# Sliding-window attention with sinks, then a highway layer: two stages turned into one pipeline over 24 blocks of 128 tokens

## The chip, the core and the metric

The kernel runs on one core of a Trainium2 chip. A core has a matrix engine (PE), a vector engine (DVE), an activation engine (ACT), a GpSimd engine (POOL) and a sync engine (SP). PE writes its results to PSUM; DVE and ACT read them there and write to SBUF. In this kernel POOL's queue issues the loads, which turn float32 in memory into fp16 in SBUF, and SP's queue issues the stores. The metric is device time in microseconds; lower is better.

## The reference

```
scores = q @ k.T / 8        # 4 batches, 8 heads, 768 positions, head size 64
keep   = (key < 4) or (0 <= query - key < 128)
a      = softmax(where(keep, scores, -1e9))
x      = (a @ v)            # heads side by side: 3072 tokens x 512
H      = relu(x @ w_h)
T      = sigmoid(x @ w_t + b_t)
out    = T * H + (1 - T) * x    # float32, 3072 x 512
```

A query sees its own block of 128 keys (lower triangle), the block before it (upper triangle) and the first four keys, the sinks.

## The kernel before

Work is done in two stages, one after the other, each with its own PSUM pools.

The attention stage loops over 4 batches and, in each, over 4 head pairs (`attention`, L142). The tiles of q and k are loaded by token block (L108, L110), turned by PE (`transpose_qk`, L124 and L126) and copied by DVE to `qTt` and `kTt` (L128, L129); the turns of the next batch are put among the head pairs of this one, and a high priority offset lets the scheduler move them to where PE has nothing else. For a head pair, `qk_mms` makes scores of two key blocks at a time, each against two query blocks of 128 (L167, 64 rows high, 256 columns); ACT takes the exponential (L176) and DVE multiplies by the mask (L179, L182, L186). `sink_scores` makes the scores against the four sinks for all later blocks (L150, four output rows) and their exponential (L153). `av_mms` then forms the weighted sum for each block and head: the block before (L198), the own block (L202) and the sinks (L206), the last one with a contraction of four rows. The value tile has a column of ones, so that the sum of the weights comes out beside the result; DVE takes its reciprocal (L227) and scales (L228) into `x_tok`. PE turns that (L235) and ACT copies it to `xT` (L236).

The highway stage (L268) loops over 24 blocks of 128 tokens. PE makes eight matmuls of 512 columns (L273 with `w_h`, L276 with `w_t`) and adds the bias with a ninth whose contraction is one row (L279). ACT takes the sigmoid (L282), DVE makes relu minus x (L284), times T (L286), plus x (L288), and SP's queue stores the tile (L289). The weights are loaded by POOL's queue (L81, L83) behind the q and k of the third batch.

Of the kernel before, what the change touches and what calls it, by code (L numbers as in the profile page):

```python
# [19 lines left out]
def kernel(  # L21
# [11 lines left out]
):  # L33
    nc = tc.nc
# [11 lines left out]
    NSC = S // P  # L46
    NHP = H // 2
    NOC = DM // P
    SCALE = 1.0 / math.sqrt(D)

    const = ctx.enter_context(tc.tile_pool(name="const", bufs=1))
    xT_pool = ctx.enter_context(tc.tile_pool(name="xTp", bufs=1))
    xT = [xT_pool.tile([P, NT], FP16, tag=f"xT{hp}", name=f"xT{hp}")
          for hp in range(NHP)]
    x_tok = xT_pool.tile([P, NT // P, NHP, P], FP16, tag="x_tok", name="x_tok")

    ident = const.tile([P, P], FP16, tag="ident")
    make_identity(nc, ident)
    ebias = const.tile([P, 1], FP32, tag="ebias")
    nc.vector.memset(ebias, _EXP_BIAS)  # L60
    masks = {}
    for nm in ("mask_std", "mask0"):
        m = const.tile([P, 2, P], FP16, tag=nm, name=nm)
        nc.gpsimd.memset(m, 1.0)
        nc.gpsimd.affine_select(
            out=m[:, 0, :], in_=m[:, 0, :], compare_op=ALU.is_ge, fill=0.0,
            base=0, pattern=[[1, P]], channel_multiplier=-1)
        nc.gpsimd.affine_select(
            out=m[:, 1, :], in_=m[:, 1, :], compare_op=ALU.is_ge, fill=0.0,
            base=-1, pattern=[[-1, P]], channel_multiplier=1)  # L70
        masks[nm] = m
    nc.vector.memset(masks["mask0"][0:NSINK, :, :], 1.0)
    wh_sb = const.tile([P, NOC, DM], FP16, tag="wh")
    wt_sb = const.tile([P, NOC, DM], FP16, tag="wt")
    bt16 = const.tile([1, DM], FP16, tag="bt16")
    ones_row = const.tile([1, P], FP16, tag="ones_row")
    nc.vector.memset(ones_row, 1.0)

    def load_weights():
        with tc.high_priority(offset=_BULK):  # L80
            nc.gpsimd.dma_start(  # L81
                out=wh_sb, in_=moe_w_h.rearrange("(kc p) of -> p kc of", p=P))
            nc.gpsimd.dma_start(  # L83
                out=wt_sb, in_=moe_w_t.rearrange("(kc p) of -> p kc of", p=P))
# [249 lines left out]
```

## Time and profile before

| | |
|---|---|
| median of 3 runs | 206.18 us (204.13 to 206.53) |
| profiled execution, span of its instructions | 204.6 us |
| mean granted PE clock, share of 2.4 GHz | 0.736 |
| instructions | 3110 |

The profiled execution is recorded from its first instruction to its last; what lies around that span isn't recorded, and the median of the runs is 1.6 us above the span. Attention takes about the first 141 us, the highway stage the rest. Busy time counts an instruction from its start to its end; matmuls overlap, so that the distance between the starts of two neighbours, and not their length, tells what one costs.

### The profile page before, as it was taken

The numbers are of one execution on the slowest core, as the hardware profiler recorded it, in microseconds if no ns is written. First come the engines' busy times: TensorE is split into PE (matmuls) and PEld (weight loads), VectorE is DVE, ScalarE is ACT, GpSimd is POOL, SyncE is SP. The second block draws the span as 40 slices with busy tenths as digits, with TensorE's granted clock in tenths as the row PEclk, the third lists the DMA queues.
The fourth block names the chain that finished last, engine by engine and source line by source line (L and its number), as shares of the span: only waits on it lengthen the run. The fifth ranks groups of instructions, "written<-read, shape, count | busy, mean of one in ns | idle before, by whom it ended". The sixth has DMA issues, their size and how long they took to land.

```text
span 204.6 us, 3110 instructions
## 1 busy us (share of the span) xinstructions
PE 180.7 (88%) x1208; PEld 92.6 (45%) x1208; DVE 114.1 (56%) x260; ACT 96.5 (47%) x106; POOL 66.8 (33%) x86
## 2 busy tenths in 40 slices
PE   0389999998999998999998989886999999998970
PEld 0255465565545556555456654443233333333320
DVE  3145276466184445554756361553078888883683
ACT  2024667555766562765764695582233223222420
POOL 8999999892999100630000000000000000000000
PEclk9999996585555555555557575555599999999997
DMA  3999999999999950590000000000004242332052
GB/s 23 116 148 147 146 147 141 139 149 85 112 147 147 173 96 0 34 122 2 0 3 0 0 2 3 0 0 0 3 33 172 105 151 106 125 131 103 0 205 104
DMA packets 79408, 16.97 MB, mean 83 GB/s; under 512 B 75297, under 2 KB 76321, under 8 KB 79394
## 3 DMA queue, kind: packets, MB, share of 16 engines
q0 software_dynamic: 75936, 10.49, 96.9%
q1 hardware_dynamic: 3458, 6.30, 8.2%
q8 instruction: 9, 0.15, 0.3%
q14 instruction: 5, 0.04, 0.1%
HBM read 20.97 MB, written 6.29 MB: 133 GB/s over the span
## 4 chain that ended last, share of the span: by engine, by line
PE 83%; DVE 4%; ACT 4%; POOL 2%; issue 2%; DMA 2%; ACTq 0%; POOLq 0%
PE sps L167 12%; PE ht L273 12%; PE ht L276 11%; PE av L198 10%; PE av L206 10%; PE av L202 6%; PE xtp L235 6%; PE tp L124 5%; PE tp L126 5%; PE ht L279 4%; PE skps L150 3%; ACT esink L153 2%; DMA ksd<-in_k_dram 2%; DVE x_tok L228 2%; ACT xT_62 L236 1%
## 5 line engine op out<-in xcount | busy, mean ns | idle before, releaser
L167 PE MATMUL sps<-qTt,kTt 64*128 64x256 f16 x192 | 32.2, 387 | 2.8 <-DVE qTt L128 1.1
L124 PE MATMUL tp<-ident,qsd 128*128 128x128 f16 x96 | 23.8, 300 | 8.6 <-DMA qsd<-in_q_dram 6.7
L282 ACT ACTIVATE tt_sb<-ht 128x512 f16<-128x512 f32 x24 | 14.3, 597 | 31.9 <-PE ht L279 31.9
L206 PE MATMUL av<-vt,esink 4*128 4x65 f16 x128 | 28.6, 223 | 0.0
L138 POOL DMA_DIRECT2D vt<-in_v_dram x24 | 21.1, 920 | 20.5 <-PE skps L150 16.4
L284 DVE SCALAR_TENSOR_TENSOR dd<-ht,x_tok 128x512 f16<-128x512 f32 x24 | 16.5, 690 | 15.8 <-ACT tt_sb L282 15.8
L126 PE MATMUL tp<-ident,ksd 128*128 128x128 f16 x96 | 23.1, 305 | 1.7 <-DMA ksd<-in_k_dram 1.7
L227 DVE RECIPROCAL rec<-av 128x6 f32<-128x6 f32 x32 | 6.1, 190 | 33.2 <-PE av L206 33.2
L110 POOL DMA_DIRECT2D ksd<-in_k_dram x24 | 23.1, 963 | 0.8 <-issue 0.5
L108 POOL DMA_DIRECT2D qsd<-in_q_dram x24 | 23.1, 961 | 0.2
L153 ACT ACTIVATE esink<-skps,ebias 4x1024 f16<-4x1024 f32 x16 | 17.6, 1098 | 9.9 <-PE skps L150 9.9
L128 DVE COPY qTt<-tp 128x512 f16<-128x512 f16 x24 | 10.0, 420 | 17.4 <-PE tp L126 17.3
L124 PEld LDWEIGHTS <-qsd 128*128 128x128 f16 x96 | 12.5, 133 | 12.8 <-DMA qsd<-in_q_dram 7.8
L228 DVE TENSOR_TENSOR x_tok<-av,rec 128x384 f16<-128x384 f32 x32 | 17.7, 552 | 0.4
L206 PEld LDWEIGHTS <-esink 4*128 4x128 f16 x128 | 12.4, 97 | 10.8
L288 DVE TENSOR_TENSOR otok<-dd,x_tok 128x512 f32<-128x512 f16 x24 | 16.3, 689 | 0.6
L235 PE MATMUL xtp<-ident,x_tok 128*128 128x128 f16 x96 | 16.6, 297 | 0.0
L126 PEld LDWEIGHTS <-ksd 128*128 128x128 f16 x96 | 12.9, 138 | 6.1 <-DMA ksd<-in_k_dram 3.1
L167 PEld LDWEIGHTS <-kTt 64*128 64x128 f16 x192 | 9.3, 107 | 12.0 <-issue 8.0
L235 PEld LDWEIGHTS <-x_tok 128*128 128x128 f16 x96 | 9.6, 131 | 6.0 <-issue 4.2
L273 PE MATMUL ht<-wh_sb,xT_61 128*128 128x512 f16 x24 | 9.7, 405 | 1.6 <-issue 1.6
L286 DVE TENSOR_TENSOR dd<-dd,tt_sb 128x512 f16<-128x512 f16 x24 | 9.9, 422 | 0.6
(350 smaller groups left out, 337.5 us busy)
## 6 DMA issues: line engine op xcount, KB each, us to landing
out_dram<-otok SPq DMA_DIRECT2D x24, 256.0 KB, 2.0
qsd<-in_q_dram POOLq DMA_DIRECT2D x24, 128.0 KB, 5.7
ksd<-in_k_dram POOLq DMA_DIRECT2D x24, 128.0 KB, 5.7
vt<-in_v_dram POOLq DMA_DIRECT2D x24, 128.0 KB, 5.3
wh_sb<-in_moe_w_h_dram POOLq DMA_DIRECT2D x1, 512.0 KB, 7.8
wt_sb<-in_moe_w_t_dram POOLq DMA_DIRECT2D x1, 512.0 KB, 9.6
bt_217<-in_moe_b_t_dram SPq DMA_DIRECT2D x1, 2.0 KB
```

Source lines behind the costliest of these rows:

```text
L108: nc.gpsimd.dma_start(out=qsd, in_=q[b, :, srange, :].transpose([1, 0, 2]))
L110: nc.gpsimd.dma_start(out=ksd, in_=k[b, :, srange, :].transpose([1, 0, 2]))
L124: nc.tensor.transpose(tp[:, j, :], qsd[:, 2 * j:2 * j + 2, :], ident)
L126: nc.tensor.transpose(tp[:, 4 + j, :], ksd[:, 2 * j:2 * j + 2, :], ident)
L138: nc.gpsimd.dma_start(out=vt[:, sc, :, 0:D], in_=v[b, :, srange, :].transpose([1, 0, 2]))
L153: nc.scalar.activation(out=esink, in_=skps, func=AF.Exp, bias=ebias[0:NSINK], scale=SCALE)
L167: nc.tensor.matmul(sps[:, hh, cc, :], lhsT=kTt[rows, hp, c * P:(c + 1) * P], rhs=qTt[rows, hp, c * P:(c + 2) * P], start=True, stop=True)
L206: nc.tensor.matmul(av_slot(hh, t), lhsT=esink[:, hh, (t - 2) * P:(t - 1) * P], rhs=vt[0:NSINK, 0, h, :], start=False, stop=True)
L228: nc.vector.tensor_tensor(out=txt[:, :, 64 * hh:64 * hh + 64], in0=av6[:, :, 0:64], in1=rec.unsqueeze(2).to_broadcast([P, NSC, 64]), op=AL ...
L235: nc.tensor.transpose(xtp[:, t, :], txt[:, t, :], ident)
L273: nc.tensor.matmul(ht[:, 0, :], lhsT=xT[kc][:, trange], rhs=wh_sb[:, kc, :], start=(kc == 0), stop=(kc == NOC - 1))
L276: nc.tensor.matmul(ht[:, 1, :], lhsT=xT[kc][:, trange], rhs=wt_sb[:, kc, :], start=(kc == 0), stop=False)
```

## The change

The two stages become one loop over 24 blocks, block n being 128 tokens with all eight heads. In iteration i, PE works in this order: scores against the sinks (every second block), scores of block i+1, weighted sum of block i, turns of q and k of block i+2, the `w_t` half of the highway layer of block i-1, turns of x of block i, the `w_h` half of block i-1. The order of PE, DVE and ACT is as written. Scores are made by block: own key block and the one before, 128 columns each, 64 rows high. The weighted sum takes 112 columns for each head (47 of them not used) into one bank of four heads. The sinks of all heads are made at full height: their keys lie in a block-diagonal tile, four matmuls add up the scores of two blocks, and one matmul for four heads adds the sink part; this is set up once for each batch. The bias is added with a tile of 128 rows of which one is not zero. The sigmoid becomes (1 + tanh(z/2))/2: the value tile's column of ones becomes 2, so that x and z come out halved, and DVE forms relu(h) - x, times (u + 1), plus 2x. ACT instead of DVE copies the turned q. q, k and v are loaded block by block, four blocks ahead; weights come behind the first two blocks. Heavily cut:

```diff
+    sd_pool = ctx.enter_context(tc.tile_pool(name="p_sd", bufs=6))
+    qkT_pool = ctx.enter_context(tc.tile_pool(name="p_qkT", bufs=5))
+    e_pool = ctx.enter_context(tc.tile_pool(name="p_e", bufs=5))
+    es_pool = ctx.enter_context(tc.tile_pool(name="p_es", bufs=2))
+    r_pool = ctx.enter_context(tc.tile_pool(name="p_r", bufs=3))
+    x_pool = ctx.enter_context(tc.tile_pool(name="p_x", bufs=4))
+    td_pool = ctx.enter_context(tc.tile_pool(name="p_td", bufs=3))
+    o_pool = ctx.enter_context(tc.tile_pool(name="p_o", bufs=4))
+    s_ps = ctx.enter_context(tc.tile_pool(name="ps_s", bufs=2, space=bass.MemoryType.PSUM))
+    av_ps = ctx.enter_context(tc.tile_pool(name="ps_av", bufs=1, space=bass.MemoryType.PSUM))
+    m_ps = ctx.enter_context(tc.tile_pool(name="ps_m", bufs=2, space=bass.MemoryType.PSUM))
...
+    def load(n):
...
+        nc.gpsimd.dma_start(out=qsd, in_=q[b, :, rows, :].transpose([1, 0, 2]))
+        nc.gpsimd.dma_start(out=ksd, in_=k[b, :, rows, :].transpose([1, 0, 2]))
...
+    load(0)
...
+        nc.vector.memset(vt, 2.0)
+    load_v(0)
+    load(1)
...
+    load_v(1)
+    nc.gpsimd.dma_start(out=wt_sb, in_=moe_w_t.rearrange("(kc p) of -> p kc of", p=P))
+    nc.gpsimd.dma_start(out=wh_sb, in_=moe_w_h.rearrange("(kc p) of -> p kc of", p=P))
...
+    def stage_T(n):
+        qsd, ksd = qk_sd.pop(n)
+        tp = m_ps.tile([P, 2 * NHP, P], FP16, tag="m", name="tp")
...
+        nc.scalar.copy(out=qT, in_=tp[:, 0:NHP, :])
+        nc.vector.tensor_copy(out=kT, in_=tp[:, NHP:2 * NHP, :])
...
+    def stage_sink_setup(b):
...
+            nc.vector.tensor_copy(out=ks3[rows, :, 4 * hh:4 * hh + NSINK],
+                                  in_=kT[rows, :, 0:NSINK])
+        vps = av_ps.tile([P, 2, 512], FP32, tag="av", name="vps")
...
+        for g in range(2):
+            nc.tensor.matmul(vps[:, g, 0:260], lhsT=sel.rearrange("p a b -> p (a b)"),
+                             rhs=vt[:, g * 260:(g + 1) * 260], start=True, stop=True)
+        vs = es_pool.tile([P, 2, 4, 65], FP16, tag="vs", name="vs")
+        for g in range(2):
+            nc.vector.tensor_tensor(
+                out=vs[:, g, :, :],
+                in0=vps[:, g, 0:260].rearrange("p (h e) -> p h e", e=65),
+                in1=bdm[:, 4 * g:4 * g + 4].unsqueeze(2).to_broadcast([P, 4, 65]),
+                op=ALU.mult)
...
+    def stage_sink(n):
...
+        sk = m_ps.tile([P, 2, P], FP32, tag="m", name="sk")
+        for t in range(2):
+            qT, _ = qkT[n + t]
+            for hp in range(NHP):
+                nc.tensor.matmul(sk[:, t, :], lhsT=ks[:, hp * P:(hp + 1) * P],
+                                 rhs=qT[:, hp, :], start=(hp == 0), stop=(hp == NHP - 1))
+        es = es_pool.tile([P, 2, P], FP16, tag="es", name="es")
+        nc.scalar.activation(out=es, in_=sk, func=AF.Exp, bias=ebias, scale=SCALE)
...
+    def stage_S(n):
...
+        for g in range(2):
+            sps = s_ps.tile([P, 2, 512], FP32, tag="s", name="sps")
+            for hl in range(2):
+                hp = 2 * g + hl
+                for pc, kk in enumerate(srcs):
                     for hh in range(2):
                         rows = slice(64 * hh, 64 * hh + 64)
+                        o = (hl * np_ + pc) * P
+                        nc.tensor.matmul(sps[:, hh, o:o + P], lhsT=kk[rows, hp, :],
+                                         rhs=qT[rows, hp, :], start=True, stop=True)
+            e = e_pool.tile([P, 2, 2, np_, P], FP16, tag="e", name="e")
+            nc.scalar.activation(out=e.rearrange("p a b c d -> p a (b c d)"),
+                                 in_=sps[:, :, 0:2 * np_ * P], func=AF.Exp,
...
+    def stage_mask(n):
...
+        for e in es:
+            ev = e.rearrange("p a b c d -> p (a b) (c d)")
+            nc.vector.tensor_tensor(
+                out=ev, in0=ev, in1=m.unsqueeze(1).to_broadcast([P, 4, np_ * P]),
+                op=ALU.mult)
...
+    def stage_A(n):
...
+        av = av_ps.tile([P, 2, 4, P], FP32, tag="av", name="av")
+        for g in range(2):
+            first = True
+            for hl in range(2):
+                for hh in range(2):
+                    h = 2 * (2 * g + hl) + hh
+                    for pc, vt in enumerate(vts):
                         nc.tensor.matmul(
+                            av[:, g, 2 * hl + hh, 0:_AVN], lhsT=es[g][:, hh, hl, pc, :],
+                            rhs=vt[:, 65 * h:65 * h + _AVN], start=first,
+                            stop=False, skip_group_check=True)
...
+            if c >= 2:
+                nc.tensor.matmul(
+                    av[:, g, :, 0:65], lhsT=es_of[n][:, c % 2, :],
+                    rhs=vs_of[b][:, g, :, :], start=False, stop=True,
+                    skip_group_check=True)
...
+        nc.vector.reciprocal(out=rec.unsqueeze(2), in_=avh[:, :, 64:65])
+        xh = x_pool.tile([P, H, D], FP16, tag="xh", name="xh")
+        nc.vector.tensor_tensor(
+            out=xh, in0=avh[:, :, 0:D],
+            in1=rec.unsqueeze(2).to_broadcast([P, H, D]), op=ALU.mult)
...
+    def stage_X(n):
+        xh = xh_of[n]
+        xtp = av_ps.tile([P, NOC, P], FP16, tag="av", name="xtp")
+        for j in range(NOC):
+            nc.tensor.transpose(xtp[:, j, :], xh[:, 2 * j:2 * j + 2, :], ident)
+        xT = x_pool.tile([P, NOC, P], FP16, tag="xT", name="xT")
+        nc.scalar.copy(out=xT, in_=xtp)
...
+    def stage_Mt(n):
...
+        tps = m_ps.tile([P, DM], FP32, tag="m", name="tps")
+        nc.tensor.matmul(tps, lhsT=ones_row, rhs=bt16, start=True, stop=False)
+        for kc in range(NOC):
+            nc.tensor.matmul(tps, lhsT=xT[:, kc, :], rhs=wt_sb[:, kc, :],
+                             start=False, stop=(kc == NOC - 1))
+        u = td_pool.tile([P, DM], FP16, tag="u", name="u")
+        nc.scalar.activation(out=u, in_=tps, func=AF.Tanh)
...
+    def stage_Mh(n):
...
+        hps = m_ps.tile([P, DM], FP32, tag="m", name="hps")
+        for kc in range(NOC):
+            nc.tensor.matmul(hps, lhsT=xT[:, kc, :], rhs=wh_sb[:, kc, :],
+                             start=(kc == 0), stop=(kc == NOC - 1))
+        dd = td_pool.tile([P, DM], FP16, tag="dd", name="dd")
+        nc.vector.scalar_tensor_tensor(out=dd, in0=hps, scalar=0.0, in1=xh,
+                                       op0=ALU.max, op1=ALU.subtract)
+        ee = td_pool.tile([P, DM], FP16, tag="ee", name="ee")
+        nc.vector.scalar_tensor_tensor(out=ee, in0=u, scalar=1.0, in1=dd,
+                                       op0=ALU.add, op1=ALU.mult)
+        otok = o_pool.tile([P, DM], FP32, tag="otok", name="otok")
+        nc.vector.scalar_tensor_tensor(out=otok, in0=xh, scalar=2.0, in1=ee,
+                                       op0=ALU.mult, op1=ALU.add)
+        nc.sync.dma_start(out=out[n * P:(n + 1) * P, :], in_=otok)
...
+    with tc.manual_schedule(engines={ENG.PE, ENG.DVE, ENG.Activation}):
+        for i in range(-2, NB + 1):
+            if 2 <= i + 4 < NB:
+                load(i + 4)
+                load_v(i + 4)
+            s = i + 1
+            if 0 <= i < NB and i % NSC >= 2 and i % 2 == 0:
+                stage_sink(i)
+            if 0 <= s < NB:
+                stage_S(s)
+            if 0 <= i < NB:
+                stage_A(i)
+            if i + 2 < NB:
+                stage_T(i + 2)
+            if 0 <= s < NB:
+                stage_mask(s)
+            if 0 <= i - 1 < NB:
+                stage_Mt(i - 1)
+            if 0 <= i < NB:
+                stage_X(i)
+            if 0 <= i < NB and i % NSC == 0:
+                stage_sink_setup(i // NSC)
+            if 0 <= i - 1 < NB:
+                stage_Mh(i - 1)
```

## Rows read from the trace of the kernel before

**Rows 1.** the page: busy time of each engine, granted clock in 40 slices
```profile
PE 180.7 (88%) x1208; PEld 92.6 (45%) x1208; DVE 114.1 (56%) x260; ACT 96.5 (47%) x106; POOL 66.8 (33%) x86
...
PEclk9999996585555555555557575555599999999997
```

**Rows 2.** the page: the chain that ended last, by engine
```profile
PE 83%; DVE 4%; ACT 4%; POOL 2%; issue 2%; DMA 2%; ACTq 0%; POOLq 0%
```

**Rows 3.** windows: stretch, length, busy PE, PEld, DVE, ACT, POOL, clock, DMA, GB/s
```profile
50.00:105.00 55.00, 53.34 (x407) 29.90 (x405) 28.87 (x73) 34.16 (x35) 22.50 (x26) 0.50 1.15 77
105.00:125.00 20.00, 18.60 (x168) 11.55 (x165) 11.05 (x27) 13.07 (x14) 0.00 (x0) 0.67 0.01 2
155.00:185.00 30.00, 30.00 (x127) 11.03 (x126) 25.18 (x43) 8.36 (x14) 0.00 (x0) 1.00 0.33 123
```

**Rows 4.** timeline of PE in attention: start us, us, instruction
```profile
108.19 0.28 PE L167 MATMUL sps<-qTt,kTt 64*128 64x256 f16 x2
108.41 0.23 PE L124 MATMUL tp<-ident,qsd 128*128 128x128 f16 x1
...
108.86 0.19 PE L202 MATMUL av<-vt,e_1378 128*128 128x65 f16 x1
108.99 0.20 PE L206 MATMUL av<-vt,esink 4*128 4x65 f16 x1
109.12 0.20 PE L198 MATMUL av<-vt,e_1358 128*128 128x65 f16 x1
```

**Rows 5.** chain in order of time, highway stage: start us, us, piece
```profile
143.19 0.43 PE ht L276
...
195.22 0.22 PE ht L273
...
195.65 0.32 PE ht L279
195.97 0.32 PE ht L273
```

**Rows 6.** groups of instructions by line, DVE: busy us, mean ns, idle before
```profile
L228 DVE TENSOR_TENSOR x_tok<-av,rec 128x384 f16<-128x384 f32 x32 | 17.7, 552 | 0.4
L284 DVE SCALAR_TENSOR_TENSOR dd<-ht,x_tok 128x512 f16<-128x512 f32 x24 | 16.5, 690 | 15.8 <-ACT tt_sb L282 15.8
L288 DVE TENSOR_TENSOR otok<-dd,x_tok 128x512 f32<-128x512 f16 x24 | 16.3, 689 | 0.6
...
L286 DVE TENSOR_TENSOR dd<-dd,tt_sb 128x512 f16<-128x512 f16 x24 | 9.9, 422 | 0.6
L129 DVE COPY kTt<-tp 128x512 f16<-128x512 f16 x24 | 9.6, 414 | 0.0
L227 DVE RECIPROCAL rec<-av 128x6 f32<-128x6 f32 x32 | 6.1, 190 | 33.2 <-PE av L206 33.2
...
L186 DVE TENSOR_TENSOR e_293<-e_293,mask_std 128x1024 f16<-128x1024 f16 x1 | 0.7, 693 | 2.3 <-ACT e_293 L176 2.3
```

**Rows 7.** timeline of DVE near the end
```profile
194.01 1.28 DVE L284 SCALAR_TENSOR_TENSOR dd<-ht,x_tok 128x512 f16<-128x512 f32 x2
...
200.49 0.69 DVE L288 TENSOR_TENSOR otok<-dd,x_tok 128x512 f32<-128x512 f16 x1
```

**Rows 8.** groups of instructions by line, ACT
```profile
L282 ACT ACTIVATE tt_sb<-ht 128x512 f16<-128x512 f32 x24 | 14.3, 597 | 31.9 <-PE ht L279 31.9
...
L282 ACT ACT_TABLE_LOAD x1 | 1.3, 1283 | 7.6 <-PE ht L279 7.6
...
L176 ACT ACTIVATE e_254<-sps,ebias 128x1024 f16<-128x1024 f32 x1 | 1.1, 1115 | 11.3 <-PE sps L167 11.3
```

**Rows 9.** the page: POOL issues, and KB each and us to landing
```profile
L108 POOL DMA_DIRECT2D qsd<-in_q_dram x24 | 23.1, 961 | 0.2
...
qsd<-in_q_dram POOLq DMA_DIRECT2D x24, 128.0 KB, 5.7
...
wt_sb<-in_moe_w_t_dram POOLq DMA_DIRECT2D x1, 512.0 KB, 9.6
```

More of the change, by code (lines that the diff above doesn't have):

```diff
@@ L49 @@
     SCALE = 1.0 / math.sqrt(D)
+    VW = H * 65 + 64
     const = ctx.enter_context(tc.tile_pool(name="const", bufs=1))
[L52 to L55, printed above, removed]
+    sd_pool = ctx.enter_context(tc.tile_pool(name="p_sd", bufs=6))
+    qkT_pool = ctx.enter_context(tc.tile_pool(name="p_qkT", bufs=5))
@@ new lines @@
+    m_ps = ctx.enter_context(tc.tile_pool(name="ps_m", bufs=2, space=bass.MemoryType.PSUM))
+    NV = 6
+    v_ring = [const.tile([P, VW], FP16, tag=f"v{i}", name=f"v{i}") for i in range(NV)]
+    qk_sd = {}
+    def load(n):
+        b, c = divmod(n, NSC)
+        rows = slice(c * P, (c + 1) * P)
+        qsd = sd_pool.tile([P, H, D], FP16, tag="qsd", name="qsd")
+        ksd = sd_pool.tile([P, H, D], FP16, tag="ksd", name="ksd")
+        nc.gpsimd.dma_start(out=qsd, in_=q[b, :, rows, :].transpose([1, 0, 2]))
+        nc.gpsimd.dma_start(out=ksd, in_=k[b, :, rows, :].transpose([1, 0, 2]))
+        qk_sd[n] = (qsd, ksd)
@@ L57, with load_v @@
+    def load_v(n):
+        b, c = divmod(n, NSC)
+        rows = slice(c * P, (c + 1) * P)
+        vt = v_ring[n % NV][:, 0:H * 65].rearrange("p (h e) -> p h e", e=65)
+        nc.gpsimd.dma_start(out=vt[:, :, 0:D], in_=v[b, :, rows, :].transpose([1, 0, 2]))
+    ebias = const.tile([P, 1], FP32, tag="ebias")
+    nc.vector.memset(ebias, _EXP_BIAS)
+    load(0)
     ident = const.tile([P, P], FP16, tag="ident")
     make_identity(nc, ident)
[L59 to L60 removed]
@@ L61 @@
[L61 to L71, printed above, removed]
@@ L72 @@
-    nc.vector.memset(masks["mask0"][0:NSINK, :, :], 1.0)
+    for vt in v_ring:
+        nc.vector.memset(vt, 2.0)
+    load_v(0)
+    load(1)
+    mask = const.tile([P, 2, P], FP16, tag="mask", name="mask")
+    nc.gpsimd.memset(mask, 1.0)
+    nc.gpsimd.affine_select(
+        out=mask[:, 1, :], in_=mask[:, 1, :], compare_op=ALU.is_ge, fill=0.0,
+        base=0, pattern=[[1, P]], channel_multiplier=-1)
+    nc.gpsimd.affine_select(
+        out=mask[:, 0, :], in_=mask[:, 0, :], compare_op=ALU.is_ge, fill=0.0,
+        base=-1, pattern=[[-1, P]], channel_multiplier=1)
@@ L231, in xtok_T @@
-            def xtok_T():
-                with tc.high_priority(offset=_BULK):
-                    xtp = tp_ps.tile([P, NSC, P], FP16, tag="tp", name="xtp")
-                    for t in range(NSC):
-                        nc.tensor.transpose(xtp[:, t, :], txt[:, t, :], ident)
-                    nc.scalar.copy(out=xT[hp][:, b * S:(b + 1) * S],
-                                   in_=xtp[:, 0:NSC, :])
-            return xtok_T
-        qk0 = load_qk_dma(0)
-        for sc in range(NSC):
-            transpose_qk(qk0, sc)
```

284 lines of the change are left out of this document (90 added, 194 removed).

## The prediction

> **What bounds the kernel now.** Read the page's busy times and clock line first: PE is busy 88% of the span, and the clock that it was granted is at half for most of the attention stage and full in most of the highway stage [rows 1]. The chain that ended last agrees: 83% of the span is PE [rows 2]. Then read the stages apart [rows 3]. From 50 to 105 us PE has work in 53.34 of 55 us, and its clock stands at 0.50 throughout, the level of 1.2 GHz. From 155 to 185 us it is busy without a gap at 1.00, the level of 2.4 GHz. DVE and ACT are busy for about half and six tenths of the first stretch, so neither bounds it. From 105 to 125 us the mean is 0.67: the clock rose for a while and fell again in the middle of the same sort of work. So the kernel is bound by PE twice over: by what PE must stream, and by the lower clock at which it streams the attention half.
>
> **PE's work in the new loop, at 2.4 GHz.** Prices are distances between starts. Eight turns of 128 columns take from 108.41 to 108.86, 0.056 us each; a pair of 64-row score matmuls of 256 columns takes 0.22 with the change to full height behind it [rows 4]. A matmul of 512 columns takes 0.22 [rows 5]. Going to a four-row matmul and back costs 0.13 each way [rows 4]; the one-row bias matmul takes 0.32 and its successor 0.32, where 0.22 would do [rows 5]. For a block with sinks, the turns of q, k and x are 12 x 0.056 = 0.67. The scores are 8 pairs at half of (0.22 - 0.11), 0.055, with two changes of height at 0.13: 0.70; if each 64-row matmul took a slot of its own, it would be 16 x 0.056 + 0.26 = 1.16, and I take the pairs, since the trace starts both of a pair together [rows 4]. The weighted sum is 16 x 0.056 = 0.90 (112 columns aren't shown; I price them as the 128 of a turn) and two of 260 columns at half of 0.22: 0.22. The sink scores are 8 x 0.056 for two blocks, 0.22 for one. The highway layer is 9 x 0.216 = 1.94, by the 0.22 less its rounding. The 128 four-row matmuls and the 24 one-row ones are gone with their changes; the latter took 0.20 us a block.
>
> That is 4.65 us. The first block of each batch has neither the earlier keys nor sinks (3.55), the second no sinks (4.22). With 16, 4 and 4 of them the mean is 4.40 us.
>
> **DVE's work.** In one iteration: reciprocal 0.19, scaling 512 columns (0.552 for 384, so 0.69), copy of k 0.41, two masks of 0.69, and dd, ee, otok [rows 6]. dd is as before, 0.69. ee was a tensor_tensor of fp16 at 0.422 and becomes a scalar_tensor_tensor of two SBUF operands, which the trace doesn't show: it lies between 0.42 and the 0.69 of dd, and I take 0.69, the row of the same operation. otok keeps two fp16 inputs and a float32 output: 0.69, by its row. The sum is 4.74 us; two independent instructions take 1.28 instead of 1.38 [rows 7], and five of the eight starts are independent, so about 4.24. The bound from below is 4.24 - 0.27 = 3.97. DVE is thus a little under PE.
>
> **ACT's work.** Two exponentials of 1024 at 1.115, tanh 0.60 by the row of the sigmoid, two copies of 512 priced at the same 0.60, and half a sink exponential (0.2): 4.2 us before overlap [rows 8]. It is covered by PE, by 0.2 us. One price decides whether it stays so. Going from the exponential to the sigmoid cost a table load of 1.28 us, once [rows 8]; if tanh needs one too, it is paid twice an iteration. [...]
>
> **What is moved, and what waits behind it.** Highway's 24 x 9 matmuls move from a stage of their own into the loop; they are PE work beside PE work, so nothing of them is hidden. What is hidden is their ACT and DVE work, which had a PE-bound stage to itself before too; no gain there. The gain is the clock of the attention half and the short matmuls. The new waits are in PE's fixed order: the turns of x stand behind scaling (0.19 + 0.69 on DVE), with the turns of q and k and the `w_t` half between (0.45 + 1.1 us of PE work) as cover; `w_h` and the next block's scores queue behind them. The scores of the next block need ACT's copy of q, made an iteration earlier. The single PSUM tile for sum and turned x makes the next weighted sum wait for ACT's copy of x; 0.87 us of `w_h` and 0.70 of scores cover its 0.60. Loads are on POOL's queue alone: 72 block loads and two of weights at 0.96 us [rows 9] are 71 us, three for a block 2.9 us, under an iteration; past the start they set nothing. Stores stay on SP's queue.
>
> **How well the queues keep pace.** Three engines with 4.2 to 4.4 us of work each can't all be hidden fully. I take the loss from the stretch of attention whose clock was partly high, where PE was busy 18.60 of 20 us [rows 3]: 4.40 / 0.93 = 4.73 us an iteration. Once in each batch the set-up of the sinks puts two small copies, two matmuls and two multiplications in one PSUM tile between x and the next weighted sum: 2 x 0.1 (an estimate, under the reciprocal's 0.19), 0.22 and 2 x 0.42 (0.69 for half the columns) are 1.3 us, exposed at worst; its bounds are 0 and 1.3, and I take 1.3, since nothing of PE's can pass it.
>
> **The start.** Iteration 0 turns block 2, whose loads stand on POOL's queue behind six block loads, the masks and both weights. Eight issues of 0.96, the next two, and about 2.5 us of constants end near 12 us; with 5.7 us to landing, k of block 2 is there at 18 us at the earliest; behind the weights' 9.6 us [rows 9] and two more loads it is 20 to 21. I take 20.5. The clock is then low, so prices double: the rest of iteration 0 (turns of q, k and x) 1.3, iteration 1 without sinks 2 x 4.22 - 0.26 = 8.2 (the changes of height don't double), and DVE's 2.07 for dd, ee and otok: the first tile is done at 32.1 us (27 to 33).
>
> **The sum.** 32.1 + 23 x 4.73 + 3 x 1.3 + the tail. The tail from the end of the last DVE instruction (200.49 + 0.69) to the end of the span (204.6) is 3.4 us [rows 7]. That is 32.1 + 108.8 + 3.9 + 3.4 = 148.2 us against a span of 204.6; the median of the runs lies 1.6 above the profiled span, so 149.8, rounded to 150. From below: 23 x 4.40 with no loss and no exposed set-up, first tile at 27: 27 + 101.2 + 3.4 + 1.6 = 133; I don't believe three engines without any loss and set the low end at 137. The score matmuls at 1.16 would add 23 x 0.46 / 0.93 = 11.
>
> **Rivals.** First, the clock stays at 1.2 GHz in the loop. From 50 to 105 us PE had almost no gap and the clock didn't rise [rows 3], so being busy isn't enough, and the loop still has turns and 64-row matmuls. Against it: of 4.65 us, 1.94 are the 512-column matmuls beside which the clock stood at 2.4 for 30 us [rows 3], and another 1.3 are now full height. Price: 2 x (4.40 - 0.26) + 0.3 = 8.6 us an iteration, over the 0.97 of the stretch at 1.2 is 8.9, so 32.1 + 23 x 8.9 + 2 + 3.4 + 1.6 = 244 us. It makes the kernel slower once more than (206 - 150) / (244 - 150) = 0.6 of the iterations run so. Chance 0.10. [...]
>
> Second, DVE's new operations cost double. If an operation that reads two SBUF operands with a scalar takes a second pass over 512 columns (L288 less L286, 0.267 us, is half a pass [rows 6]), ee and otok take 1.22 each: 4.24 + 1.07 = 5.31, over 0.93 5.7, and 32.1 + 131 + 3.9 + 5 = 172 us. Against it: L288 reads two fp16 SBUF operands at one pass. Chance 0.09. [...]
>
> Third, the queues wait for each other. If PE stands for reciprocal and scaling (0.88) and its own drain (a turn lasts 0.23 [rows 4]) in each iteration, because DVE is still at the block before: 4.73 + 1.1 = 5.83, and 149.8 + 25 = 175 us. Chance 0.13.
>
> Fourth, tables alternate. ACT has 4.2 + 2 x 1.28 = 6.8 us, over 0.93 7.3: 32.1 + 168 + 3.9 + 5 = 209; without loss 197. Chance 0.03.
>
> Last, the change wouldn't do what it says if loads held the loop. At 71 us for all of them block 23 would have landed by 80, and iteration 21 would need it after 125. Not in the count but for the start.
>
> **How the numbers follow.** Forecast 0.62, clock 0.10, DVE 0.09, queues 0.13, tables 0.03, below 137 us 0.03. The range takes in the forecast with its bounds, the DVE and the queue case: 137 to 177; what is left out is 0.16. About 2% is what a measurement tells here. Faster by more: 0.62 + 0.09 + 0.13 + 0.03 + half of the tables' 0.03, 0.88; within 2%: the other half, 0.02; slower: 0.10, the clock.
>
> **What would show it.** The profile after should have one kind of stretch from about 32 us on, a granted clock of 1.00, 4.7 us between stores, and PE, DVE and ACT all over 80% busy. Turns and 112-column matmuls should start 0.056 us apart, score pairs likewise, the bias matmul 0.22 from its neighbour. ee at 0.69 and a single table load would close two rivals. A clock at 0.50 in the loop, or PE idle for DVE once an iteration, would make the forecast wrong.

## The result and the profile after

The changed kernel takes 145.16 us (median of 4 runs, 144.66 to 145.69) where the kernel before takes 206.36 beside it: 0.705 of the time, with a 95% interval of 0.700 to 0.710. The profiled execution was the fastest of the four: it took 144.66 us, 1.7 above its span of 143.0, as far above as before. The forecast was 150 in a range of 137 to 177.

Read first, as before, the page's busy times, the granted clock and the chain that ended last.

```profile
PE 114.4 (80%) x1312; PEld 73.8 (52%) x1312; DVE 114.1 (80%) x228; ACT 90.3 (63%) x129; POOL 66.8 (47%) x86
...
PEclk9999999999999999999999999999999999999996
...
DVE 36%; PE 32%; ACT 10%; DMA 7%; issue 7%; POOL 6%; DVEq 0%; POOLq 0%
```

Beside [rows 1] PE has 66 us less busy time, and the span is 61.6 us shorter; DVE has the same 114.1 us in both kernels. The chain that was 83% PE [rows 2] is now shared by DVE and PE, with more steps from one engine to another than long stretches of one. Up to about 28 us the clock row can't be taken at its word: it reads 9 there, in [rows 1] too, yet at 26 us the turns of 128 columns start 0.107 us apart in both kernels, and in the loop 0.056. By the starts the clock is low up to about 28 us. The middle of the loop by windows (columns as in [rows 3]) shows how close the engines stand.

```profile
60.00:120.00 60.00, 56.26 (x681) 36.61 (x679) 55.28 (x108) 46.22 (x67) 23.67 (x27) 1.00 1.15 117
```

PE is busy for 0.94 of this stretch at a granted clock of 1.00, where attention had 0.97 at 0.50 [rows 3], DVE for 0.92, ACT for 0.77.

The groups by line, DVE and then ACT, answer to [rows 6] and [rows 8] (line numbers are those of the changed kernel):

```profile
L316 DVE SCALAR_TENSOR_TENSOR ee<-u,dd 128x512 f16<-128x512 f16 x24 | 16.6, 692 | 2.9 <-ACT es L214 0.5
...
L313 DVE SCALAR_TENSOR_TENSOR dd<-hps,xh 128x512 f16<-128x512 f32 x24 | 16.5, 687 | 3.4 <-PE hps L310 3.4
L177 DVE COPY kT<-tp 128x512 f16<-128x512 f16 x24 | 10.0, 418 | 12.0 <-ACT qT L176 12.0
```

```profile
L234 ACT ACTIVATE e<-sps,ebias 128x1024 f16<-128x1024 f32 (+1 forms) x48 | 47.4, 1039 | 15.7 <-PE sps L231 11.4 <-ACT xT L288 4.2
...
L176 ACT ACT_TABLE_LOAD x1 | 1.3, 1283 | 0.8 <-PEq L363 0.8
```

ee (692 ns) costs what dd does (687) although it reads SBUF alone, and there is one table load in the whole run. Now PE's own order in one iteration without sink scores and the start of one with them (timeline of PE: start us, us, instruction):

```profile
62.60 1.02 PE L310 MATMUL hps<-wh_sb,xT 128*128 128x512 f16 x4
63.55 0.62 PE L231 MATMUL sps<-qT,kT 64*128 64x128 f16 x16
64.11 0.22 PE L262 MATMUL av<-v_93,e 128*128 128x112 f16 x1
64.17 0.21 PE L262 MATMUL av<-v_94,e 128*128 128x112 f16 x1
...
65.14 0.39 PE L171 MATMUL tp<-ident,qsd 128*128 128x128 f16 x4
...
65.58 0.38 PE L296 MATMUL tps<-bt_136,ones_row 128*128 128x512 f16 x1
65.80 1.03 PE L298 MATMUL tps<-wt_sb,xT 128*128 128x512 f16 x4
66.77 0.40 PE L286 MATMUL xtp<-ident,xh 128*128 128x128 f16 x4
67.15 1.02 PE L310 MATMUL hps<-wh_sb,xT 128*128 128x512 f16 x4
```

One round takes 67.15 - 62.60 = 4.55 us. The bias is 0.22 ahead of its neighbour, the eight turns of q and k take 0.44, the 112-column matmuls start 0.05 apart, and all 16 score matmuls fit into 0.56 us.

The stores' last operation, otok (L319), starts at 31.07 us for the first block and at 138.89 for the last. From the second batch on, two of them lie 5.0 us apart where the iteration holds sink scores, 4.5 to 4.55 where it doesn't, and 5.58 where the sinks are set up; the last three distances are 4.41, 4.41 and 2.12.

### The profile page after: what moved, and what is told of

It reads as the page before. It is cut to its first block, busy times and chain, and to the rows that moved or that the text cites. A ratio compares the mean times of both kernels' runs of the same rounds, so it can differ in the third digit from the quotient of the medians.

```text
span 143.0 us, 3308 instructions
## 1 busy us (share of the span) xinstructions
PE 114.4 (80%) x1312; PEld 73.8 (52%) x1312; DVE 114.1 (80%) x228; ACT 90.3 (63%) x129; POOL 66.8 (47%) x86
## 3 DMA queue, kind: packets, MB, share of 16 engines
q1 hardware_dynamic: 3458, 6.30, 12.7%
## 4 chain that ended last, share of the span: by engine, by line
DVE 36%; PE 32%; ACT 10%; DMA 7%; issue 7%; POOL 6%; DVEq 0%; POOLq 0%
PE hps L310 12%; DMA ksd<-in_k_dram 7%; DVE ee L316 6%; DVE otok L319 6%; DVE e L247 6%; DVE dd L313 5%; ACT e L234 5%; DVE xh L277 5%; PE av L262 4%; PE tps L298 4%; PE xtp L286 3%; DVE kT L177 3%; PE sk L211 3%; ACT qT L176 2%; DVE vs L196 2%
## 5 line engine op out<-in xcount | busy, mean ns | idle before, releaser
L234 ACT ACTIVATE e<-sps,ebias 128x1024 f16<-128x1024 f32 (+1 forms) x48 | 47.4, 1039 | 15.7 <-PE sps L231 11.4
L298 PE MATMUL tps<-wt_sb,xT 128*128 128x512 f16 x96 | 25.1, 384 | 0.0
L310 PE MATMUL hps<-wh_sb,xT 128*128 128x512 f16 x96 | 24.6, 378 | 0.6
L176 ACT COPY qT<-tp 128x512 f16<-128x512 f16 x24 | 14.0, 585 | 14.1 <-PE tp L173 14.1
L262 PEld LDWEIGHTS <-e 128*128 128x128 f16 x352 | 20.4, 100 | 4.2 <-DVE vs L196 1.2
L247 DVE TENSOR_TENSOR e<-e,mask 128x1024 f16<-128x1024 f16 x32 | 20.5, 682 | 0.0
L313 DVE SCALAR_TENSOR_TENSOR dd<-hps,xh 128x512 f16<-128x512 f32 x24 | 16.5, 687 | 3.4 <-PE hps L310 3.4
L316 DVE SCALAR_TENSOR_TENSOR ee<-u,dd 128x512 f16<-128x512 f16 x24 | 16.6, 692 | 2.9 <-ACT es L214 0.5
L319 DVE SCALAR_TENSOR_TENSOR otok<-xh,ee 128x512 f32<-128x512 f16 x24 | 16.6, 692 | 0.8
L277 DVE TENSOR_TENSOR xh<-av,rec 128x512 f16<-128x512 f32 x24 | 16.6, 691 | 0.8
L298 PEld LDWEIGHTS <-xT 128*128 128x128 f16 x96 | 9.6, 100 | 9.1 <-issue 0.8
L310 PEld LDWEIGHTS <-xT 128*128 128x128 f16 x96 | 9.2, 97 | 8.1 <-issue 1.3
L286 PEld LDWEIGHTS <-xh 128*128 128x128 f16 x96 | 6.2, 100 | 13.1 <-DVE xh L277 11.5
```

The costliest lines, as they stand in the source:

```text
L234: nc.scalar.activation(out=e.rearrange("p a b c d -> p a (b c d)"), in_=sps[:, :, 0:2 * np_ * P], func=AF.Exp, bias=ebias, scale=SCALE)
L247: nc.vector.tensor_tensor(out=ev, in0=ev, in1=m.unsqueeze(1).to_broadcast([P, 4, np_ * P]), op=ALU.mult)
L262: nc.tensor.matmul(av[:, g, 2 * hl + hh, 0:_AVN], lhsT=es[g][:, hh, hl, pc, :], rhs=vt[:, 65 * h:65 * h + _AVN], start=first, stop=False, ...
L277: nc.vector.tensor_tensor(out=xh, in0=avh[:, :, 0:D], in1=rec.unsqueeze(2).to_broadcast([P, H, D]), op=ALU.mult)
L298: nc.tensor.matmul(tps, lhsT=xT[:, kc, :], rhs=wt_sb[:, kc, :], start=False, stop=(kc == NOC - 1))
L310: nc.tensor.matmul(hps, lhsT=xT[:, kc, :], rhs=wh_sb[:, kc, :], start=(kc == 0), stop=(kc == NOC - 1))
```

## The experiments

The theory at the outset was the prediction's: PE's work over a loss of 0.07, at a clock that the loop keeps up. The rivals were a clock that needs highway's long matmuls, DVE as the bound, and a round trip over several engines. All changes are against the changed kernel, each alone unless said. "After" below is its 145.16 us.

**1. Highway in a stage of its own.** What is the pipelining worth, and does the clock need it?

```diff
-    x_pool = ctx.enter_context(tc.tile_pool(name="p_x", bufs=4))
+    x_pool = ctx.enter_context(tc.tile_pool(name="p_x", bufs=24))
...
-            if 0 <= i - 1 < NB:
-                stage_Mt(i - 1)
...
-            if 0 <= i - 1 < NB:
-                stage_Mh(i - 1)
+        for n in range(NB):
+            stage_Mt(n)
+            stage_Mh(n)
```

> The highway matmuls leave the loop and get a loop of their own behind it, as before the change; full-height sinks and bias, block order and tanh stay. Theory A: the 512-column matmuls in each iteration are what keeps the clock at 2.4 GHz; without them the attention loop is granted 0.50 for most of its time. PE then has 2 x (4.65 - 1.94) = about 5.4 us an iteration, and the median is 185 to 200 us. Theory B: doing away with the four-row matmuls is enough for the clock. Then attention runs at 1.00 and is bound by ACT at about 3.5 us an iteration, the highway loop by PE or DVE at about 2.1 us: 20 + 22 x 3.6 + 24 x 2.1 + 5 = 155 us.

Measured 173.52 us, 0.850 of before [0.843, 0.857]. Windows of attention, of its middle and of highway:

```profile
25.00:115.00 90.00, 67.01 (x1011) 53.41 (x1009) 57.80 (x123) 68.27 (x94) 45.83 (x53) 0.92 1.29 83
55.00:95.00 40.00, 28.93 (x480) 22.61 (x479) 26.29 (x57) 33.80 (x47) 23.67 (x27) 1.00 1.51 97
120.00:165.00 45.00, 44.60 (x193) 18.54 (x192) 41.99 (x64) 12.56 (x22) 0.00 (x0) 1.00 0.32 123
```

Neither theory holds as a whole: B has the clock and not the time. The clock stands at 1.00 for 40 us of attention alone, with PE busy for 28.93 of 40 us and no 512-column matmul beside it; outside of these 40 us it was lower at times, hence 0.92 in the mean of the 90. So the clock can stay high without the highway. Yet 28.4 us of the gain are gone: attention alone has no engine near full (67.01, 57.80 and 68.27 of 90 us), because its steps wait for each other, and highway alone is DVE's, end to end, as its chain shows:

```profile
130.35 0.61 DVE dd L313
...
131.78 0.69 DVE otok L319
132.47 0.61 DVE dd L313
```

That is 2.12 us a block. PE's 44.60 us in that window count instructions that overlap; its nine matmuls of a block start 0.22 apart, 1.94 us, and then wait for dd. Beside each other, the one's work fills the other's waits.

**2. Sigmoid in place of tanh** (the same values by another table).

```diff
-        nc.scalar.activation(out=u, in_=tps, func=AF.Tanh)
+        nc.scalar.activation(out=u, in_=tps, func=AF.Sigmoid, scale=2.0)
...
-        nc.vector.scalar_tensor_tensor(out=ee, in0=u, scalar=1.0, in1=dd,
-                                       op0=ALU.add, op1=ALU.mult)
+        nc.vector.scalar_tensor_tensor(out=ee, in0=u, scalar=2.0, in1=dd,
+                                       op0=ALU.mult, op1=ALU.mult)
```

> tanh becomes the sigmoid of twice its argument, with the one multiplication behind it adapted, so that the result is the same. Theory A, by the one table load of the kernel before: two loads of 1.28 us in each iteration, ACT at 3.5 + 2.6 = 6.1 us or more becomes the bound, and the run takes 180 to 209 us with 48 or so table loads. Rival: loads are hidden in ACT's idle time or not needed; then 145 to 150 us.

Measured once: 182.81 us. The groups of ACT:

```profile
L301 ACT ACT_TABLE_LOAD x22 | 28.2, 1283 | 0.4
L234 ACT ACT_TABLE_LOAD x13 | 16.7, 1283 | 8.3 <-issue 8.1
...
L214 ACT ACT_TABLE_LOAD x8 | 10.3, 1283 | 0.1
```

With one at L176 there are 44 loads; at 1.28 us they are 56 us, and the run is 37.7 us longer than after. Tanh is no detail of this change: in the old order of stages one load ahead of the highway was enough [rows 8]; where an exponential and a sigmoid alternated, it was nearly two an iteration (44 in 24).

**3. The bias by one row again, and 4. the weighted sum with 65 columns.** A little more and a little less work for PE.

```diff
-        nc.tensor.matmul(tps, lhsT=ones_row, rhs=bt16, start=True, stop=False)
+        nc.tensor.matmul(tps, lhsT=ones_row[0:1, :], rhs=bt16[0:1, :], start=True, stop=False)
```

> The bias matmul has one row again instead of 128; the result is the same. Its price on PE is 0.20 us a block by the kernel before. Theory A: an iteration takes what the larger of PE (4.88 with sink scores, 4.43 without) and DVE (4.46) needs. Then the 8 iterations with sink scores grow by 0.20 and the others by up to 0.17: 1.6 to 4 us more, 147 to 149 us. Theory B: the iteration is a chain from ACT's exponentials over its copy of q and DVE's copy of k to the matmuls of w_h, on which the bias doesn't lie: less than 0.7 us more.

```diff
-_AVN = 112
+_AVN = 65
```

> The weighted sum takes 65 columns a head instead of 112, none of them unused; the result is the same. Theory A: the clock doesn't hang on the unused columns; it stays at 1.00, and PE saves 16 x (0.05 - 0.04) = 0.16 us an iteration, of which only those with sink scores see something: 143 to 145.5 us. Theory B: the unused columns are what keeps PE at 2.4 GHz; without them the clock falls in at least part of the loop and the run takes over 152 us.

The bias row: 145.66 us, 0.712 [0.703, 0.721]. 65 columns: 145.05, 0.709 [0.703, 0.715]. The distances between stores are the same as after's within 0.1 us in both. Windows of the first and the second:

```profile
60.00:120.00 60.00, 57.80 (x684) 36.69 (x682) 55.32 (x108) 45.86 (x67) 23.68 (x27) 1.00 1.15 117
```

```profile
60.00:120.00 60.00, 53.02 (x700) 33.23 (x700) 55.24 (x108) 45.81 (x67) 23.68 (x27) 1.00 1.16 119
```

PE's busy time rose by 1.5 us in the one and fell by 3.2 in the other, and nothing came of either. The order shown for after tells why: in that round of 4.55 us PE waits 0.11 us ahead of the turns of x, for the scaling (66.77, though the `w_t` half leaves room at 66.66), and 0.14 behind them, for DVE's copy of k out of the PSUM buffer that `w_h` takes. Its own order needs 4.30. In run 3 the bias costs 0.21 more from start to start, and the two waits shrink from 0.25 to 0.05. PE's sum of work, though busy for 0.94 of the time, is not what bounds the loop. The clock stays at 1.00 without the unused columns too (second window).

**5. k's copy before q's.** In after's chain the copy of k (DVE) begins only when ACT's copy of q, behind the exponentials, has ended (0.03 us after it in 17 of 24), though they read different halves of one PSUM tile.

```diff
+        nc.vector.tensor_copy(out=kT, in_=tp[:, NHP:2 * NHP, :])
         nc.scalar.copy(out=qT, in_=tp[:, 0:NHP, :])
-        nc.vector.tensor_copy(out=kT, in_=tp[:, NHP:2 * NHP, :])
```

> DVE's copy of k is written ahead of ACT's copy of q, nothing else. In the changed kernel DVE's copy starts when ACT's ends, though the two read different halves of the tile. Theory A: iterations with sink scores (5.0 us) are the chain exponentials 2.12, copy of q 0.58, copy of k 0.44, matmuls of w_h 1.0, sink scores 0.46, scores to the next exponential 0.3; without the copy of k in it they fall to what PE needs, 4.6 to 4.9, and those without (4.5) stay, since DVE's sum is 4.46. 8 x 0.1 to 0.4 is 1 to 3 us less: 142 to 144.5 us. Theory B: PE's sum bounds the iterations with sink scores; nothing changes, 145 us.

154.64 us, 0.753 [0.742, 0.764]: both theories missed. One of the copies still waits for the other; only now it is ACT's, and it hangs on DVE's order. One round of its chain (start us, us, piece):

```profile
61.96 0.70 DVE dd L313
...
64.33 0.69 DVE xh L277
65.03 0.34 DVE kT L176
...
65.39 0.59 ACT qT L177
...
66.03 1.04 PE hps L310 x4
...
67.09 0.70 DVE dd L313
```

From dd to dd this is 5.13 us, and each iteration of the loop takes 5.12 but for the set-ups (6.3 to 7.3) and the last three.

**6. The turns of q and k ahead of the scores.**

```diff
+            if i + 2 < NB:
+                stage_T(i + 2)
             if 0 <= s < NB:
                 stage_S(s)
             if 0 <= i < NB:
                 stage_A(i)
-            if i + 2 < NB:
-                stage_T(i + 2)
```

> The turns of q and k of block i+2 go ahead of the scores of block i+1 on PE, so that ACT copies q before the exponentials and not behind them, and DVE copies k before the masks' block. Theory A (the chain through ACT's queue sets the iterations with sink scores): the copies leave the chain, PE waits for nothing before the matmuls of w_h, and these iterations fall from 5.0 to 4.6 to 4.9; the exponentials start 0.45 us later. 141 to 145 us. Theory B: the place of the copies doesn't matter, 145 us; or the later exponentials cost up to 0.45 an iteration, 155 us.

151.26 us, 0.737 [0.729, 0.746]; 5.36 us with sink scores, 4.75 without. The turns of x have lost part of their cover (the weighted sum is now right ahead of the `w_t` half) and wait for the scaling:

```profile
PEld L286 <- DVE xh L277: 19.8, 24, 1.4
```

That is once in every iteration (us in total, times, longest); in after the same wait comes to 11.5 us in 16 times.

**7. Loads of blocks 2 and 3 ahead of the weights.**

```diff
+    load(2)
+    load_v(2)
+    load(3)
+    load_v(3)
     nc.gpsimd.dma_start(out=wt_sb, in_=moe_w_t.rearrange("(kc p) of -> p kc of", p=P))
...
-            if 2 <= i + 4 < NB:
+            if 4 <= i + 4 < NB:
```

> The loads of blocks 2 and 3 are put ahead of the two weights on POOL's queue. Theory A, by the step on the start (block 2's turns wait for loads that stand behind the weights; they start at 19.1 us): those turns start near 12 us, the first tile is done 3 to 6 us sooner, and the rest is unchanged: 139 to 142 us. Rival: the weights then land so late that the matmuls of w_t, which stood at 26.6 us, wait for them: no gain or up to 3 us lost.

140.12 us, 0.683 [0.675, 0.691]; the first otok starts at 25.70 instead of 31.07, and the distances between stores are the same. Block 2's turns of q on PE, after's timeline first, then this kernel's:

```profile
19.10 0.61 PE L171 MATMUL tp<-ident,qsd 128*128 128x128 f16 x4 [5.74 <-DMA qsd<-in_q_dram]
```

```profile
13.19 0.63 PE L175 MATMUL tp<-ident,qsd 128*128 128x128 f16 x4
```

**8. One more DVE operation of 0.69 us in each iteration,** behind otok, into a tile that nothing reads.

```diff
+        spare = td_pool.tile([P, DM], FP16, tag="spare", name="spare")
+        nc.vector.scalar_tensor_tensor(out=spare, in0=u, scalar=1.0, in1=dd,
+                                       op0=ALU.add, op1=ALU.mult)
```

> DVE repeats one operation of 0.69 us (0.61 from start to start) in each iteration into a tile that nobody reads; the output is the same. Theory A: DVE with 4.46 us of work bounds the iterations without sink scores (4.50 to 4.55), so these grow by 0.6, those with sink scores (5.0) by 0.1: 14 x 0.6 + 8 x 0.1 = 9 us, 154 us. Theory B: all iterations are a chain over ACT, in which DVE has room: less than 3 us more, under 148 us.

156.16 us, 0.760 [0.750, 0.771]: 5.0 to 5.1 us an iteration with or without sink scores (6.13 at the set-up). In the loop its chain is DVE almost without a gap (dd at 68.12 us, the next at 73.22), the addition in it with 0.60:

```profile
70.24 0.60 DVE spare L322
```

So DVE's own order takes some 4.5 us of an iteration, and where no sink scores are it had nothing to spare. That doesn't make it the only bound; run 11 asks from the other side.

**9. The `w_t` half ahead of the turns of q and k.** The `w_h` matmuls then take the PSUM buffer of the `w_t` half and needn't wait for the copies.

```diff
-            if i + 2 < NB:
-                stage_T(i + 2)
             if 0 <= s < NB:
                 stage_mask(s)
             if 0 <= i - 1 < NB:
                 stage_Mt(i - 1)
+            if i + 2 < NB:
+                stage_T(i + 2)
```

> The w_t half is issued before the turns of q and k instead of behind them, so that the w_h matmuls take over the PSUM buffer of the w_t half instead of that of the turns; all work is as it was. Theory A (in iterations with sink scores, 5.0 us, the cycle runs through that buffer: exponential, ACT's copy of q, DVE's copy of k, w_h, next sink scores): the copies leave the cycle, and iterations with sink scores fall to about 4.7 to 4.9 us; those without stay at 4.46 to 4.55, DVE's own sum: 142 to 144.5 us. Theory B (the cycle is closed by something else, or the turns, now later, hold back the copies): 145 us or more, and the sink iterations stay at 5.0.

144.1 us, 0.707 [0.702, 0.712]. The total is where theory A put it (142 to 144.5), but not by its reason: the iterations with sink scores take 5.22 to 5.26, those between 4.34 to 4.47, in the mean no less than before (from first to last otok 108.3 us against 107.8). What is saved is 2.1 us of the start (first otok at 28.96). The wait has moved and isn't gone: the sink scores now take the buffer of the turns, and PE stands ahead of them until DVE has copied k.

```profile
65.87 0.35 DVE kT L177
...
66.26 0.61 PE sk L211 x8
```

So this run doesn't tell what the loop would be without that wait.

**10. Sink sums of half height.** Eight matmuls of 64 rows and 65 columns in place of two of 128 rows and 260.

```diff
-            if c >= 2:
-                nc.tensor.matmul(
-                    av[:, g, :, 0:65], lhsT=es_of[n][:, c % 2, :],
-                    rhs=vs_of[b][:, g, :, :], start=False, stop=True,
-                    skip_group_check=True)
+                    if c >= 2:
+                        half = slice(64 * g, 64 * g + 64)
+                        nc.tensor.matmul(
+                            av[:, g, 2 * hl + hh, 0:65], lhsT=es_of[n][half, c % 2, :],
+                            rhs=vs_of[b][half, g, 2 * hl + hh, :], start=False,
+                            stop=False, skip_group_check=True)
```

> In the 16 blocks with sinks, the two full-height matmuls of 260 columns over the sinks become eight of 64 rows and 65 columns, one behind each head's own matmuls, so that PE changes height 16 times a block more, as the kernel before did with four rows. Theory A (a change costs 0.13 us each way, as in the kernel before): 16 x 0.13 = 2.1 us more PE work less 0.22 - 0.06 saved, in iterations of 4.75 on average: about 6.5 us each where sinks are, 165 to 180 us in all; full height is then what gave much of the gain. Theory B (the changes are hidden or cheaper at the full clock): below 155 us.

166.9 us, 0.818 [0.812, 0.824]. The timeline of PE, with one head's share from 72.09 to 72.43:

```profile
72.09 0.20 PE L269 MATMUL av<-vs,es 64*128 64x65 f16 x1
72.23 0.27 PE L262 MATMUL av<-v,e 128*128 128x112 f16 x2
72.43 0.20 PE L269 MATMUL av<-vs,es 64*128 64x65 f16 x1
```

0.34 us a head, where two 112-column matmuls take 0.10: the small matmul with its two changes of height costs 0.24, at the full clock. Eight of them less the 0.22 that they replace are 1.7 us, and the iterations with the sums grew by 1.25 to 1.5 (to 5.76, 5.98 and 6.43). Theory A's range holds, at its lower end. The granted clock of the loop is 1.00, so changes of height don't lower it here.

**11 and 12. One copy of q and k on ACT,** alone, and with the loads of run 7.

```diff
-        qT = qkT_pool.tile([P, NHP, P], FP16, tag="qT", name="qT")
-        kT = qkT_pool.tile([P, NHP, P], FP16, tag="kT", name="kT")
-        nc.scalar.copy(out=qT, in_=tp[:, 0:NHP, :])
-        nc.vector.tensor_copy(out=kT, in_=tp[:, NHP:2 * NHP, :])
-        qkT[n] = (qT, kT)
+        qk = qkT_pool.tile([P, 2 * NHP, P], FP16, tag="qk", name="qk")
+        nc.scalar.copy(out=qk, in_=tp)
+        qkT[n] = (qk[:, 0:NHP, :], qk[:, NHP:2 * NHP, :])
```

> ACT copies the turned q and k out of PSUM in one instruction of 1024 columns (about 1.04 us, by the exponential of as many) in place of 0.59 on ACT and, behind it, 0.42 on DVE; nothing else changes. DVE then has about 4.0 us an iteration, ACT 4.1, PE 4.45. Theory A (DVE's sum sets the iterations without sink scores): those fall from 4.5 to about 4.3 to 4.4, where PE's sum is, those with sink scores to 4.65 to 4.8: 141 to 143.5 us. Theory B (the chain exponential, copies, w_h matmuls, sink scores, exponential sets the time; it is as long with one copy of 1.04 as with 0.48 and 0.44 in a row): 144.5 to 147 us.

> The one copy on ACT together with the loads of blocks 2 and 3 ahead of the weights (which alone gave 140.12 us). Theory A: 136 to 138.5 us. Theory B: 139.5 to 142 us.

Alone 143.15 us, 0.698 [0.694, 0.702]; with the loads 139.99, 0.682 [0.677, 0.686], no better than run 7 (its first otok starts at 27.15 us, 1.45 later), as theory B had it. Runs 7 and 12 are the fastest versions of this study. Windows of 84 us in the loop, run 7's and then that of the copy alone:

```profile
40.00:124.00 84.00, 78.44 (x944) 50.44 (x941) 77.59 (x152) 64.13 (x92) 31.55 (x36) 1.00 1.16 121
```

```profile
40.00:124.00 84.00, 78.35 (x943) 50.58 (x941) 72.58 (x135) 70.28 (x94) 34.19 (x39) 1.00 1.22 124
```

DVE has 5 us less to do in 84 and the iterations take 4.95, 4.47 and 4.41 us instead of 5.0, 4.55 and 4.5, with 5.67 instead of 5.58 at the set-up; from first to last otok that is 0.7 us of 108 (the rest of the 2.0 is a start 0.8 earlier and the spread of runs). So DVE's sum isn't by itself what bounds the loop either: 0.3 us less of it a round gave back 0.03. The total lies in A's range, but the loop hardly moved, as B had it.

**What does bound it** is not one engine. A first bound is seen in after's last iterations, where DVE has no masks and no copy, PE no scores, and an interval is still 4.41 us. The chain there:

```profile
130.83 0.70 DVE dd L313
...
132.35 0.69 DVE otok L319
...
133.20 0.70 DVE xh L277
...
134.34 0.88 PE hps L310 x4
...
135.25 0.70 DVE dd L313
```

and between scaling (xh) and the `w_h` matmuls, in PE's timeline:

```profile
133.95 0.40 PE L286 MATMUL xtp<-ident,xh 128*128 128x128 f16 x4 [0.94 <-DVE xh L277]
```

This is a round trip: the `w_h` matmuls release dd; DVE's fixed order puts dd, ee and otok of one block ahead of reciprocal and scaling of the next; the turns of x wait for the scaling, and the next `w_h` matmuls stand behind them. 135.25 - 130.83 = 4.42 us, and PE stands idle for 0.94 of it. After's chain goes round the same way in full iterations too, at times: dd at 73.29 us, the next dd at 77.70. In others DVE's own order stands as long: in a round without sink scores DVE (timeline) goes from dd to dd without waiting for another engine.

```profile
63.66 0.69 DVE L313 SCALAR_TENSOR_TENSOR dd<-hps,xh 128x512 f16<-128x512 f32 x1
...
68.21 0.69 DVE L313 SCALAR_TENSOR_TENSOR dd<-hps,xh 128x512 f16<-128x512 f32 x1
```

That is 4.55 us, 0.14 more than the round trip, and PE's own order is 4.30. Cutting DVE's or PE's work by itself returned next to nothing (run 11's copy 0.7 us of 108, run 4's 65 columns 0.1 of the time): the next bound stands right behind.

Why iterations with sink scores take 5.0 is read from the chain alone, from one `w_h` half to the next:

```profile
57.68 0.95 PE hps L310 x4
58.63 0.46 PE sk L211 x8
...
60.51 1.11 ACT e L234
61.61 0.48 ACT qT L176
...
62.12 0.44 DVE kT L177
...
62.60 1.02 PE hps L310 x4
```

The sink scores bring ACT a third exponential, and behind it stand the other two and both copies: 4.92 us. Run 11's one copy takes 0.91 in the chain where the two took 0.48 and 0.44, so that chain stayed as long (4.95), and in run 9 the wait for the copy moved to the sink scores. No run has shortened the chain, so that it sets the 5.0 is not shown by experiment. Issuing the scaling ahead of ee and otok, which would cut the round trip, wasn't tried.

## Why the prediction was right, point by point

**The sum.** Measured from the same trace: first tile at 31.8 us (31.07 + 0.69), 107.8 to the last, tail 143.0 - 139.6 = 3.4. Forecast were 32.1, 112.7 and 3.4. The 4.9 us between them are these: the last interval is 2.12, not 4.73, since block 23 is left with highway alone (2.6); the set-up of the sinks costs 5.58 - 4.5 = 1.08 and not 1.3, three times (0.7); the other 22 intervals are 4.66 in the mean instead of 4.73 (1.6). The profiled execution took 1.7 us more than its span, where 1.6 was taken; the median of the four is another 0.5 above it.

**PE's work.** 4.43 without sink scores was forecast and 4.55 found: the scores cost less (0.66 with both changes of height, for 0.70; the 64-row matmuls do go in pairs) and the weighted sum too (1.03 for 1.12); the `w_t` half, the turns of x and `w_h` cost more (0.97, 0.38 and 0.95 for 0.86, 0.22 and 0.86), for the turns wait 0.11 for the scaling, the first `w_h` matmul 0.14 for the copy of k, and the first change of height, 0.1, lies between the last `w_h` matmul and the scores. So PE's own work is less than forecast, 4.30, and the rest is waiting. Sink scores add 0.46, as two times 0.22 had it.

**DVE's and ACT's work.** ee at 0.69 was right. In the window DVE has 55.28 / 60 of a mean iteration of 4.85 (a batch of six takes 29.1, its set-up in it), 4.47 us, where 4.24 was taken without the set-up. In the round shown, five starts of eight are hidden, as taken, but by some 0.08 us each and not 0.1, and the three operations that need the result of their neighbour start 0.17 late in all: 4.55 in order. DVE isn't a little under PE, as the prediction had it, but above it. ACT has 3.7, not 4.2, so the expectation that it would be over 80% busy was wrong (0.77), without effect.

**The loss.** 0.93 was taken from a stretch of the old attention [rows 3] and 0.938 came out, but the reason given, that three engines of nearly equal work hide each other badly, is too vague: runs 3, 4 and 11 show that no one engine's sum decides. What the loss stood for is the round trip, DVE's order and the chain over ACT; that a ratio from another stage, at another clock, gave 4.73 where 4.66 was measured is in part luck. The rival of the queues had the mechanism, PE standing for reciprocal and scaling; it missed that the other work covers nearly all of that, so that it sets a floor of 4.41 and not 5.83 us. With an order changed, the scaling is in the loop's way again, in run 5's chain and in run 6's longest wait of PE.

**"No gain there" was the step that failed.** The prediction held that moving highway into the loop hides nothing new, because its DVE and ACT work lay beside a PE-bound stage before. At the new prices that is wrong: with the full clock, neither stage is PE's any more (run 1's windows and chain), and run 1 puts 28.4 of the 61.2 us on the move itself. The total was right because the sum per iteration was made for the loop as it is; the account of where the gain comes from was not. The other 32.8 us come from the rest of the change, without the move; run 10 shows that eight small matmuls of 64 rows in place of two full ones cost 21.7 at the full clock, number and height together. How much of the 32.8 is the clock and how much the short matmuls, no run tells. These pieces overlap and aren't to be added up.

**The clock.** It rose, and that rival is closed for this loop: 1.00 in all windows from 28 to 140 us. What kept it low before stays open: runs 1, 4 and 10 show that, taken one at a time, the high clock needs neither the highway beside attention nor the 112 columns, and that changes of height at 64 rows don't lower it (1.00 in run 1's window from 55 to 95 us and in those of runs 4 and 10 from 60 to 120); four-row matmuls in this loop weren't tried. Turns don't exclude it either: 12 of them in each iteration stood beside a clock of 1.00. The traces give the clock as a share of full speed alone; the prediction's 2.4 and 1.2 GHz are its 1.00 and 0.50, and as frequencies an estimate from the columns started in a nanosecond: 512 in 0.216 us (2.4) in the highway stage before, 128 in 0.107 (1.2) in its attention.

**DVE's double price and the tables.** ee at 692 ns closes the one: with a second pass it would have been 1.22 us, by the author's estimate. It takes what dd takes from PSUM (687 ns), while the old tensor_tensor of the same shape and types took 422 [rows 6]; why, no run shows. No run of the kernel before shows whether tanh needs a load of its own, and the forecast's 4.2 us for ACT has none; in after, exponential and tanh came with one load of 1.28 us in the whole run, and in run 2 sigmoid and exponential with 44. The price of the tables' rival was 197 to 209 us, and run 2 took 182.8: ACT's own work is 3.7 us where 4.2 was taken, and 44 loads came in 24 iterations where two in each were taken, 3.7 + 1.83 x 1.28 = 6.1 instead of 6.8.

**The start.** Block 2's turns start at 19.10 us, 20.5 was taken; from there to the first tile it took 12.7 where 11.6 was taken, so two misses nearly cancel. The reason was right, and run 7 shows what it is worth: 5.0 us, by the order of the loads alone. The low clock of the start was right too, by the starts: four turns take 0.43 us up to about 28 us and 0.22 in the loop.

## What to carry to other kernels

When the engines of a pipeline stand within a few per cent of each other, sum the round trips as well as the engines: follow one released buffer or tile through each engine's fixed order back to itself, and look at the last iterations, where the round trip stands bare. A move that hides nothing at the old prices must be costed again at the new ones. Where a short operation joins a loop, ask what else it brings: a table load (1.28 us here), a change of height (two of them and a matmul of 65 columns 0.24 us in run 10), a place in front of a load on a queue (5.0 us in run 7).

## What was unexpected

Two engines that read different halves of one PSUM tile ran one after the other here: in after, DVE's copies of k had 12.0 us of idle time ahead of them, all behind ACT's copies of q, and with the order exchanged ACT waited 31.7 us for DVE. The program's own waits set that order: in after's trace all 24 copies of k wait for a semaphore that only ACT's instructions raise, and not for PE's; with the order exchanged the copies of q wait for DVE's (24 of 24). What the two would do without these waits, no run shows.

A small matmul of 64 rows and 65 columns between full-height ones cost 0.24 us at a granted clock of 1.00, with the change of height on either side, more than a full-height one of 512 columns (0.22).
